# A planned kernel: from the fifth FFN unit on, the planner takes each weight block to land later

## Chip, cores, metric

One core of one Trainium2 chip runs the whole program in one launch. The metric is the device time of a run in microseconds (us); the time before is the median of three timed runs.

## The reference, cut to what matters

Three stages run on a tensor of 2 batches x 768 positions: windowed attention with sink tokens (8 heads of 64), then a mixture of four attention experts, then the stage that this change touches, a feed-forward mixture of eight experts that sends every position to one expert:

```python
logits = x @ w_gate                      # (2, 768, 8)
e      = routed expert of (b, s)         # argmax, or the previous position's expert by a local gate
h      = maximum(x[b, s] @ w1[e], 0)     # 512 -> 1024
out[b, s] = softmax(logits[b, s])[e] * (h @ w2[e])   # 1024 -> 512
```

## The kernel before

**The FFN stage.** The 1536 positions are sorted by expert into units of 128 rows, counted from 0. On this input, twelve units do the work: an expert has full units, and remainders of up to 32 rows go into one mixed batch (the pieces, `qw` weights, L1741). The twelve units belong to three experts: one has units 0 to 5, one has unit 6, one has units 7 to 11. Unit u does the following:

- a gather brings its rows (`xg`, L1563), TensorE transposes them (L1543), ScalarE and VectorE write them as `ux` in a high part (L1546) and a low part (L1550);
- its weights come as eight blocks of 512 KB, named (c, hf): c = 0, 1 are the two column halves of w1, c = 2, 3 the two row halves of w2, hf is the half of each. A block is loaded into its own `raw` buffer (`ld`, L1492, issued by SyncE, SP). Each of the eight has exactly one buffer, so unit u's load of a block waits until unit u-1's copy of it was split. The load is conditional: where unit u has the expert of unit u-1, nothing is moved and only the issue remains, so after unit 1 only units 6 and 7 move weights;
- every block is split: `hi` (ScalarE, L1507) rounds it to a high part, `lo` (VectorE, L1515) subtracts to get the low part; the split is done again in every unit. The results lie in eleven `w` buffers (their trace names are those of the tensors that once lived there: `w`, `wo_h`, `xT`, `wqk_h`, `wvg_h`);
- `unit_first`: 24 matmuls (three for each product, L315 to L317) into two banks, ScalarE's relu of each bank to `hs` (L1603), TensorE's transposes of `hs` (L1543), and high and low part of those, `hT` (L1546, L1550). These, with the output's scaling below, are a unit's evacuations: work that brings results out of PSUM;
- `unit_second`: 24 matmuls on `hT` with the c = 2, 3 blocks, ScalarE's scaling to `yo` (L1638), and a scatter to the output by GpSimd (L1641).

**What sets the order.** Tile's scheduler is off. Every piece of work is a `Task` with an engine, a duration, dependencies, buffers to acquire and release, and a priority (100 u plus an offset). `Order.run` is a list scheduler that works while the program is built: it asks `Order.ready` for the earliest start of each task, puts out the one that starts first (among equals the one with the lowest priority number), and advances that engine's clock. What it puts out is each engine's instruction order on the chip; its times are used for nothing else. `ready` takes the end of each dependency plus a latency; for a load (engine "DMA") the latency is 2.0, and a conditional load itself counts as `CLD` = 0.4:

```python
LAT = {"PE": 0.20, "ACT": 0.155, "DVE": 0.14, "POOL": 0.18, "DMA": 2.0, ...}
K["ld", u, c, hf] = add("DMA", CLD if u > 1 else 1.46, f, acq=[(("raw", 2 * c + hf), ...)], ...)
```

So the planner believes a block ready for its `hi` 2.4 after its load could start, whether or not the load moves anything. Units up to 10, and the front of unit 11, are one list; from unit 11 on, each unit is planned inside a branch on the number of units.

Of the kernel before, what the change touches and what calls it, by code (L numbers as in the profile page):

```python
# [32 lines left out]
RL = 1  # L33
PRP = 20
BPR = 120
BSP = 60
LAG1 = 0
ESP = 0.85
# [23 lines left out]
QN = 4  # L62
# [1 line left out]


class Task:
    __slots__ = ("eng", "dur", "fn", "deps", "acq", "rel", "prio", "end", "name", "rows", "fills", "lat")

    def __init__(self, eng, dur, fn, deps, acq, rel, prio, rows=False):
        self.eng, self.dur, self.fn, self.prio, self.rows = eng, dur, fn, prio, rows  # L70
        self.deps = [d for d in deps if d is not None]
        self.acq, self.rel = list(acq), list(rel)
        self.end = None
        self.fills = False
        self.lat = None


class Order:
# [17 lines left out]
    def add(self, eng, dur, fn, deps=(), acq=(), rel=(), prio=0, rows=False):  # L96
        t = Task(eng, dur, fn, deps, acq, rel, prio, rows)
        self.tasks.append(t)
        return t

    def ready(self, t):
        e = self.free.get(t.eng, 0.0)
        if t.eng == "PE" and t.rows != self.rows:
            e += self.TURN
        for d in t.deps:
            if d.end is None:
                return None
            e = max(e, d.end + (self.SAME.get(t.eng, 0.0) if d.eng == t.eng else d.lat or self.LAT[d.eng]))
        kinds = [a[0] for a in t.acq]
        for tag in set(kinds):  # L110
            free = sorted(x for x in self.slots.setdefault(tag, [0.0] * len(self.bufs[tag])) if x is not None)
            n = kinds.count(tag)
            if len(free) < n:
                return None
            e = max(e, free[n - 1])
        return e
# [54 lines left out]
def d_mr(n):  # L171
    return (n * 0.4375 + 8 if n >= 256 else 213) / 1000
# [14 lines left out]
def d_v(n):  # L187
    return (n / 0.96 + 65) / 1000


def d_a(n, extra=0):
    return (n / 1.2 + 52 + 93 * extra) / 1000
# [11 lines left out]
def fused_kernel(  # L204
# [106 lines left out]
    def f32(ap):  # L311
        return ap.bitcast(F32)
# [46 lines left out]
    if sinks:  # L359
# [4 lines left out]
        for r in range(3):  # L364
            t = bdm[32 * r:32 * r + 32]
# [1062 lines left out]
    def inv():  # L1428
        for j in range(T):
# [3 lines left out]
                   prio=END)  # L1433
# [4 lines left out]
        rel=["r_in"])  # L1438

    def spread(key, i):  # L1440
# [7 lines left out]
        rel=["r_q"])  # L1448
# [50 lines left out]
    def sp(u, c, hf, pr=None, ahead=False):  # L1499
        pool = (c, hf) in POOLW and u > 0 or ahead  # L1500
        pr = 100 * u + 5 * c + hf if pr is None else pr

        def hi():
            if ahead:
                nc.scalar.activation(R["w", u, c, hf][0], R["raw", u, c, hf], AF.Copy)
            else:
                nc.scalar.activation(R["w", u, c, hf][0], R["raw", u, c, hf], AF.Copy)  # L1507

        def lo():
            wh, wl = R["w", u, c, hf]  # L1510
            eng = nc.gpsimd if pool else nc.vector
            for k in range(PARTS if pool else 1):
                w_ = 512 // (PARTS if pool else 1)
                s_ = slice(k * w_, (k + 1) * w_)
                eng.tensor_sub(wl[:, :, s_], R["raw", u, c, hf][:, :, s_], f32(wh)[:, :, s_])  # L1515
        after = [K["ga", 1]] if u == 0 and (c, hf) == (3, 1) else []
        h = K["wh", u, c, hf] = add("ACT", d_a(1024) + 0.055, hi, deps=[K["ld", u, c, hf]] + (spent + [K["routed", JE]] * c if ahead else [K.get(("wh", 0, 1, 1))] * (u == 0 and c == 2)),
                                    acq=[("w", ("w", u, c, hf))], prio=pr)
        K["wl", u, c, hf] = add("POOL" if pool else "DVE", 2.4 + 0.07 * (PARTS - 1) if pool else d_v(1024), lo,
                                deps=[h] + after, prio=pr,  # L1520
                                rel=[("raw", u, c, hf)])
# [36 lines left out]
    def unit_front(u):  # L1558
        bp = base(u)

        def ga():
            xg = R["xg", u]
            nc.gpsimd.indirect_dma_start(out=xg, out_offset=None, in_=x2d if u else x2d[:JE * C, :],  # L1563
                                         in_offset=bass.IndirectOffsetOnAxis(ap=gix[:, u:u + 1] if u else gix0, axis=0))
        g0 = K["ga", u] = fo.add("POOL", 1.4, ga, deps=[K["gix"]] + [K["out", j] for j in range(T)] + [K.get("eui")] * (u > 1) if u else [K["gix0"]] + [K["out", j] for j in range(JE)] + [K["turnover"]],
                    acq=[("xg", ("xg", u))], prio=bp - 50 if u else at2((JE - 1) // NT, (JE - 1) % NT, E1) + RPO + 6)
        if u == 1:

            K["eui"] = fo.add("POOL", 0.1, lambda: nc.gpsimd.tensor_copy(eui[:32 + PC], euf[:32 + PC]), deps=[K["euf"], g0], prio=-49)
        for c in range(4 if u else 0):  # L1570
            for hf in range(2):
                ld(u, c, hf)
        g1 = fo.add("GD", 0.0 if u else 0.8, lambda: None, deps=[g0], prio=bp - 50)
        K["ux", u] = tr(("ux", u), lambda j: R["xg", u][:, j * 128:(j + 1) * 128], "ux", KD,
                        [g1] + ([K["g1", 0]] if u == 1 else []), bp - 40, [("xg", u)])
        for c in range(2 if u else 0):
            for hf in range(2):
                sp(u, c, hf)

    def unit_first(u):  # L1580
# [27 lines left out]
        for c in range(2, 4):  # L1608
            for hf in range(2 if u or c == 2 else 1):
                sp(u, c, hf, bp + 5 * c + hf + BSP if u else bp + 5 * c + hf - 48)  # L1610

    def unit_second(u, halves_=(0, 1)):
# [3 lines left out]
        for n in halves_:  # L1616
            for j0 in range(0, 4, step):
                def g2(n=n, j0=j0):
                    hh, hl = R["hT", u, n]
                    for j in range(j0, j0 + step):  # L1620
# [4 lines left out]
                g2s.append(fo.add("PE", 3 * step * d_mr(512), g2, deps=[K["hT", u, n], K["wl", u, 2 + n, hf]] + g2s,  # L1625
                                  acq=() if g2s else [("B", ("yp", u))], prio=bp + BPR + 4 * n + hf,
                                  rel=([("w", u, 2 + n, hf)] if (j0 + step) % 2 == 0 else []) + ([("hT", u, n)] if j0 + step == 4 else [])))
# [4 lines left out]
    def unit_end(u):  # L1632
# [7 lines left out]
        def sc_():  # L1640
# [5 lines left out]
            last_sc.append(sct)  # L1646
        e_ = fo.add("ACT", d_a(512), ev, deps=g2s + [K.get("pu")], acq=[("yo", ("yo", u))], rel=[("yp", u)], prio=bp + BPR + 10)
        f_ = fo.add("POOL", 1.1, sc_, deps=[e_], prio=bp + BPR + 10)
        fo.add("GD", 0.0, lambda: None, deps=[f_], rel=[("yo", u)], prio=bp + BPR + 10)

    n_ = len(order.tasks)
    unit_front(0)
    for c in range(4):
        if c == 1:
            behind = [K["ga", 0]]
        elif c == 2:
            behind = [K["ga", 0], K["out", T - DEFER]]
        for hf in range(2):
            ld(0, c, hf, END + c)
            if c < 2:  # L1660
                sp(0, c, hf, END + 40, True)
# [203 lines left out]
```

## Time and profile before

| | us |
|---|---|
| three timed runs: median (lowest to highest) | 424.39 (423.37 to 425.52) |
| the profiled execution: its time | 427.42 |
| its span, first to last instruction | 425.6 |
| outside the span | 1.8 |

TensorE has work for 403.8 us of the span, VectorE 336.2, ScalarE 326.6, GpSimd 173.6. The profiled execution is 3.0 us longer than the median of the timed runs. The FFN units fill the span from about 236 us to its end. A timeline row gives start, length, engine, line, what is written and read, and in brackets how long the engine stood idle before it and what ended that. Ends of matmuls are modelled: one that is followed at once by the next shows 0.39 us and starts 0.23 us before the next.

### The profile page before, as it was taken

What the parts mean: (1) busy time and instruction counts of PE and PEld (TensorE: products, weight loads), DVE (VectorE), ACT (ScalarE), POOL (GpSimd) and SP (SyncE); (2) the same over time, 40 slices, a digit from 0 to 9 for tenths busy, and PEclk for the clock granted to TensorE, in tenths of its full rate; (3) what the DMA queues carried; (4) which work ended last, traced back from release to release, by engine and by line L of the source; (5) the groups of instructions that cost most, each with busy time, mean ns of one, the idle gap of its engine ahead of it and who ended that gap; (6) DMA issues with size and microseconds to landing.
All of it is one profiled execution on the core that took longest, in us unless ns stands there. A gap on an engine that the chain in (4) does not pass through costs nothing.

```text
span 425.6 us, 10370 instructions
## 1 busy us (share of the span) xinstructions
PE 403.8 (95%) x3322; PEld 316.1 (74%) x3322; DVE 336.2 (79%) x959; ACT 326.6 (77%) x767; POOL 173.6 (41%) x270
## 2 busy tenths in 40 slices
PE   7899999999999997999999999999999699999994
PEld 3579979978779867979767677556566488888883
DVE  3999598697898789588799879476886779898690
ACT  5799799679999697765796438477695978989780
POOL 8289995198886358401642043111020401100101
PEclk9999999999999999999999999999999979999999
DMA  9997288645978445220910247786658971100011
GB/s 181 170 203 197 67 154 159 122 101 101 180 111 160 101 89 111 52 75 13 339 74 27 74 153 267 245 244 203 202 168 261 393 296 46 49 27 26 24 28 55
DMA packets 102046, 59.03 MB, mean 139 GB/s; under 512 B 84319, under 2 KB 85855, under 8 KB 101984
## 3 DMA queue, kind: packets, MB, share of 16 engines
q1 hardware_dynamic: 99824, 51.47, 48.7%
q0 software_dynamic: 2160, 6.82, 4.6%
q8 instruction: 28, 0.46, 0.5%
q14 instruction: 34, 0.28, 0.2%
HBM read 86.58 MB, written 6.55 MB: 219 GB/s over the span
## 4 chain that ended last, share of the span: by engine, by line
PE 49%; issue 24%; DVE 18%; POOL 4%; ACT 3%; SPq 1%; POOLq 0%; another core or an unknown queue 0%; DMA 0%; ACTq 0%; DVEq 0%
PE bank L315 8%; PE bank L317 8%; PE bank L316 8%; PE bank L685 6%; DVE P L699 4%; PE bank L809 3%; PE bank L1741 3%; PE bank L410 3%; DVE pT L816 2%; DVE PX L699 2%; POOL out_dram L1641 2%; PE bank L1140 1%; PE bank L1543 1%; PE bank L780 1%; PE bank L826 1%
## 5 line engine op out<-in xcount | busy, mean ns | idle before, releaser
L1515 DVE TENSOR_TENSOR w<-raw,w 128x1024 fp32r<-128x1024 f32 x44 | 52.9, 1221 | 13.8 <-ACT w L1507 13.6
L709 ACT ACTIVATE P<-P,nm 128x260 f32<-128x260 f32 (+3 forms) x100 | 53.1, 535 | 10.9 <-DVE nm L699 10.6
L1507 ACT ACTIVATE w<-raw 128x1024 fp32r<-128x1024 f32 x44 | 45.8, 1062 | 9.6 <-DMA raw<-in_moe_w_dram 8.3
L769 POOL TENSOR_TENSOR raw<-PX,raw 128x512 f16<-128x512 f32 (+2 forms) x34 | 35.5, 1050 | 15.8 <-ACT raw L764 13.9
L1641 POOL DMA_INDIRECT out_dram<-yof,six x12 | 13.0, 1085 | 67.4 <-ACT yof L1638 66.2
L816 DVE TENSOR_TENSOR pT<-bank,pT 128x512 f16<-128x512 f32 (+1 forms) x50 | 30.7, 631 | 9.4 <-ACT pT L812 9.3
L1563 POOL DMA_INDIRECT xgf<-x2d,gix x9 | 10.4, 1152 | 66.3 <-PE bank L1543 60.8
L685 PE MATMUL bank<-kT,qT 64*128 64x260 f32 (+1 forms) x192 | 31.5, 398 | 2.1 <-POOL kT L583 1.1
L709 ACT ACTIVATE PX<-PX,nm 128x260 f32<-128x260 f32 (+4 forms) x60 | 30.5, 510 | 1.4 <-DVE nm L699 1.3
L315 PE MATMUL bank<-xT,wqk_h 128*128 128x256 f32 x96 | 29.5, 307 | 0.0
L410 PE MATMUL bank<-ident,raw 128*128 128x128 f32 x168 | 28.0, 289 | 0.5 <-DVE raw L949 0.3
L812 ACT ACTIVATE pT<-bank 128x512 f16<-128x512 f32 (+1 forms) x50 | 26.1, 550 | 2.8 <-PE bank L809 2.5
L809 PE MATMUL bank<-ident,P 128*128 128x128 f32 x180 | 26.8, 277 | 1.0 <-ACT P L709 0.7
L317 PE MATMUL bank<-xT,wqk_l 128*128 128x256 f32 x96 | 27.8, 289 | 0.0
L316 PE MATMUL bank<-xT,wqk_h 128*128 128x256 f32 x96 | 27.7, 288 | 0.0
L699 DVE CUSTOM_DVE_ANT_0 P<-bank,mask 128x260 f32<-128x260 f32 (+1 forms) x60 | 22.3, 399 | 5.4 <-POOL mask L332 4.7
L685 PEld LDWEIGHTS bank<-kT,qT 64*128 64x128 f32 x192 | 19.2, 185 | 9.2 <-issue 2.3
L1603 ACT ACTIVATE hs<-bank 128x512 f32<-128x512 f32 x24 | 14.3, 596 | 15.3 <-PE bank L317 15.3
L646 POOL TENSOR_SCALAR raw<-raw,s_sv 128x256 f32<-128x256 f32 x20 | 18.4, 930 | 18.0 <-ACT qT L416 9.1
L410 PEld LDWEIGHTS bank<-ident,raw 128*128 128x128 f32 x168 | 20.1, 162 | 7.0 <-DVE nm L699 2.0
L685 PE MATMUL bank<-k,q 64*128 64x256 f32 (+3 forms) x128 | 24.4, 466 | 0.1
L1515 DVE TENSOR_TENSOR xT<-raw,xT 128x1024 fp32r<-128x1024 f32 x16 | 19.2, 1217 | 6.6 <-ACT xT L1507 6.4
(456 smaller groups left out, 1476.8 us busy)
## 6 DMA issues: line engine op xcount, KB each, us to landing
raw<-in_moe_w_dram SPq DMA_DIRECT2D x104, 512.0 KB
qw<-in_moe_w_dram SPq DMA_DIRECT2D x64, 256.0 KB
raw<-in_v_dram SPq DMA_DIRECT2D x12, 256.0 KB
x2d<-x SPq DMA_DIRECT2D x12, 256.0 KB
raw<-in_q_dram SPq DMA_DIRECT2D x11, 256.0 KB
raw<-in_k_dram SPq DMA_DIRECT2D x11, 256.0 KB
pT<-raw SPq DMA_TRANSPOSE x46
raw<-in_moe_wv_dram SPq DMA_DIRECT2D x1, 512.0 KB
```

What stands on the lines that cost most here:

```text
L315: nc.tensor.matmul(o, l[0], r[0], start=start, stop=False)
L316: nc.tensor.matmul(o, l[0], r[1], start=False, stop=False)
L317: nc.tensor.matmul(o, l[1], r[0], start=False, stop=stop)
L410: nc.tensor.transpose(p[:, j * 128:(j + 1) * 128], src(j), ident)
L685: nc.tensor.matmul(o, l, r, start=True, stop=True)
L699: nc.vector.tensor_tensor_reduce(p, s, sg["mask"], 0.0 if dead and st == 1 else -scale, gr["nm"] if si else 3.0e38, op0=OP.add, op1=OP.min ...
L709: nc.scalar.activation(p, p, AF.Exp, bias=gr["nm"], scale=-1.0, accum_out=sg["sum"]())
L769: nc.gpsimd.tensor_sub(shaped(pl[:, s_], dims), p_, shaped(ph[:, s_], dims))
L809: nc.tensor.transpose(R[tk][:, j * 128:(j + 1) * 128], R[gr["P"]][:, c:c + 128], ident)
L816: nc.vector.tensor_sub(pl[:, :n * 128], R[tk][:, :n * 128], ph[:, :n * 128])
L1507: nc.scalar.activation(R["w", u, c, hf][0], R["raw", u, c, hf], AF.Copy)
L1515: eng.tensor_sub(wl[:, :, s_], R["raw", u, c, hf][:, :, s_], f32(wh)[:, :, s_])
```

## The change

A task gets a new field, `slack`, which `ready` adds to the end of each of its dependencies. It is 0 for all tasks but the `hi` of the weight blocks of units 5 and up (`QN` is 4), where it is 6.0; a `hi` has one dependency, its load. So the planner now counts such a block as ready 8.4, and not 2.4, after its load could start. No instruction is added or removed, and no wait: only the order in which the planner puts them out can differ.

```diff
+LATE = 6.0
...
+        self.slack = 0.0
...
-            e = max(e, d.end + (self.SAME.get(t.eng, 0.0) if d.eng == t.eng else d.lat or self.LAT[d.eng]))
+            e = max(e, d.end + t.slack + (self.SAME.get(t.eng, 0.0) if d.eng == t.eng else d.lat or self.LAT[d.eng]))
...
         h = K["wh", u, c, hf] = add("ACT", d_a(1024) + 0.055, hi, deps=[K["ld", u, c, hf]] + ..., prio=pr)
+        if u > QN:
+            h.slack = LATE
```

## Rows read from the trace of the kernel before

**Rows 1.** The page's busy time, share of the span, instructions.
```profile
PE 403.8 (95%) x3322; PEld 316.1 (74%) x3322; DVE 336.2 (79%) x959; ACT 326.6 (77%) x767; POOL 173.6 (41%) x270
```

**Rows 2.** Busy time by stretch: engines, then granted clock, DMA share, GB/s.
```profile
312.50:325.00 12.50, 12.50 (x68) 8.99 (x66) 12.25 (x12) 10.82 (x14) 2.60 (x2) 1.00 0.65 208
...
329.90:339.10 9.20, 6.16 (x29) 4.38 (x28) 7.07 (x8) 8.79 (x12) 3.60 (x3) 1.00 1.05 393
339.10:346.00 6.90, 6.26 (x15) 4.96 (x16) 5.13 (x6) 4.65 (x6) 0.87 (x1) 0.51 1.05 393
346.00:358.40 12.40, 12.40 (x62) 10.18 (x61) 11.28 (x11) 10.48 (x14) 2.00 (x2) 1.00 0.33 119
...
383.20:395.60 12.40, 12.40 (x62) 10.20 (x61) 11.29 (x12) 11.16 (x15) 0.98 (x1) 1.00 0.06 22
```

**Rows 3.** TensorE's timeline, units 4 to 6, 315 to 355 us.
```profile
315.25 0.60 PE L1543 MATMUL bank<-ident,xgf 128*128 128x128 f32 x4
...
319.12 0.40 PE L315 MATMUL bank<-wo_h,uxf 128*128 128x512 f32 x1
...
324.64 0.60 PE L1543 MATMUL bank<-ident,hs 128*128 128x128 f32 x4
325.17 1.92 PE L1741 MATMUL bank<-qw,v2l 128*32 128x512 f32 x16
...
331.25 0.66 PE L1543 MATMUL bank<-ident,hs 128*128 128x128 f32 x4 [1.18 <-ACT hs L1603]
...
338.35 0.50 PE L315 MATMUL bank<-wo_h,ux 128*128 128x512 f32 x1 [1.83 <-ACT ux L1546]
...
339.74 0.80 PE L317 MATMUL bank<-wo_h,ux 128*128 128x512 f32 x1 [0.67 <-DVE ux L1550]
...
346.13 0.39 PE L317 MATMUL bank<-w,ux 128*128 128x512 f32 x1
...
354.65 0.39 PE L315 MATMUL bank<-w,uxf 128*128 128x512 f32 x1
```

**Rows 4.** ScalarE's timeline, 322 to 338 us.
```profile
322.72 0.60 ACT L1603 ACTIVATE hs<-bank 128x512 f32<-128x512 f32 x1
326.60 1.06 ACT L1507 ACTIVATE wo_h<-raw 128x1024 fp32r<-128x1024 f32 x1 [3.28 <-DMA raw<-in_moe_w_dram]
329.65 1.06 ACT L1507 ACTIVATE w<-raw 128x1024 fp32r<-128x1024 f32 x1 [1.99 <-DMA raw<-in_moe_w_dram]
330.62 0.58 ACT L1603 ACTIVATE hs<-bank 128x512 f32<-128x512 f32 x1
...
332.98 1.06 ACT L1507 ACTIVATE w<-raw 128x1024 fp32r<-128x1024 f32 x1 [0.28 <-DMA raw<-in_moe_w_dram]
...
337.70 0.60 ACT L1546 ACTIVATE ux<-bank 128x512 fp32r<-128x512 f32 x1
```

**Rows 5.** ScalarE's timeline, 314 to 317 us: unit 5's first splits.
```profile
314.09 1.05 ACT L1507 ACTIVATE wo_h<-raw 128x1024 fp32r<-128x1024 f32 x1
...
315.99 0.68 ACT L1638 ACTIVATE yof<-bank,pu 128x512 f32<-128x512 f32 x1
```

**Rows 6.** VectorE's timeline: low parts of units 5 and 6.
```profile
315.63 1.22 DVE L1515 TENSOR_TENSOR wo_l<-raw,wo_h 128x1024 fp32r<-128x1024 f32 x1
...
327.70 1.23 DVE L1515 TENSOR_TENSOR wo_l<-raw,wo_h 128x1024 fp32r<-128x1024 f32 x1 [2.30 <-ACT wo_h L1507]
```

**Rows 7.** SP's load issues for units 6 and 7, in three windows.
```profile
321.33 2.60 SPq L1492 DMA_DIRECT2D raw<-in_moe_w_dram  x3
...
324.35 3.96 SPq L1492 DMA_DIRECT2D raw<-in_moe_w_dram  x5
...
333.67 2.54 SPq L1492 DMA_DIRECT2D raw<-in_moe_w_dram  x3
```

**Rows 8.** ScalarE's timeline, splits of units 7 and 8.
```profile
340.07 1.07 ACT L1507 ACTIVATE w<-raw 128x1024 fp32r<-128x1024 f32 x1
...
368.58 1.06 ACT L1507 ACTIVATE wqk_h<-raw 128x1024 fp32r<-128x1024 f32 x1 [0.30 <-PE bank L317]
```

More of the change, by code (lines that the diff above doesn't have):

```diff
@@ L66 @@
 class Task:
-    __slots__ = ("eng", "dur", "fn", "deps", "acq", "rel", "prio", "end", "name", "rows", "fills", "lat")
+    __slots__ = ("eng", "dur", "fn", "deps", "acq", "rel", "prio", "end", "name", "rows", "fills", "lat", "slack")
     def __init__(self, eng, dur, fn, deps, acq, rel, prio, rows=False):
```

## The prediction

> **What bounds the kernel now.** I read the page first: TensorE has work for 95% of the span [rows 1]. Then the table by stretch [rows 2], cut at unit boundaries counted back from the twelve output scalings: TensorE is full from 312 us to 325 and again from 346 to the tail, where a unit takes 12.40 us, all of it TensorE. The exception is 329.9 to 346: first 6.16 us of work in 9.20, then a stretch at a granted clock of 0.51, the lower of the two levels (1.2 of 2.4 GHz). Third, TensorE's timeline there [rows 3]: three waits, 1.18 for a relu, 1.83 and 0.67 for `ux`, all for ScalarE or for VectorE behind it. Fourth, ScalarE's timeline [rows 4]: why these are late. Unit 5's second relu reads a bank that is complete when TensorE goes on to the transposes at 324.64 [rows 3], yet it starts at 330.62. ScalarE stands 3.28 and 1.99 us at the heads of unit 6's splits of blocks (0, 0) and (0, 1), whose loads have not landed. The relu, `hT` (its transposes done since 325.2) and later `ux` are queued behind them. The weights are late and the evacuations are not; the order makes both late.
>
> **Part 1, the order of unit 6's splits.** The planner puts `hi` of block (0, 0) of unit 6 ahead of the second relu, because it counts the load as 0.4 + 2.0. On the chip, the load is issued at 321.33 [rows 7] and its split starts at 326.60: 5.3 us instead of 2.4. With 8.4 the `hi` becomes ready in the plan after the second relu, both `hT` high parts and the pieces' output, which take two to five planned us; so I expect ScalarE to have, in this order: relu 1 of unit 5, the rest of unit 5's splits, relu 2, `hT` 1, the pieces' scaling, `hT` 2, then unit 6's (0, 0), (0, 1), (1, 0) with unit 4's scaling and `ux` between. What this removes:
> - the three waits, 1.18 + 1.83 + 0.67 = 3.68 us [rows 3]. By the modelled ends each hides another 0.16 (a matmul's row lasts 0.39, the next starts after 0.23), which would make it 4.2;
> - the half clock. From 339.74 to 346.13 TensorE starts 15 matmuls [rows 2, 3]: 6.39 us. At the 0.23 us between starts of the full stretches (24 matmuls of unit 5 in 5.52 us, 319.12 to 324.64) they are 3.47. The difference is 2.92 us, and it goes if the clock fell because of the three waits right ahead of it.
>
> Gross 3.68 + 2.92 = 6.60, with the hidden part 7.1 at most.
>
> The Trainium skill (TensorE: Matmul & The Clock Gate, section "Why this matters for your kernels") lays the fall to the lower clock on a long idle gap between bursts of matmuls. The longest here is 1.83 us and matmuls run between the three, so I doubt that it would call these the cause; by that rule the clock's 2.92 would stay lost, and the sum would be 3.68. But the clock fell at 339.10, as the third wait began [rows 2, 3], after nothing else than these waits: I go by the row.
>
> **Part 2, unit 5's splits.** They wait 6 more as well, though their loads move nothing (same expert as unit 4). Before, (0, 0), at 314.09, and (0, 1) stand ahead of unit 3's scaling at 315.99 [rows 5]. I expect scaling and `ux` first. The scaling must wait for unit 3's last matmul, which `ux`'s transposes follow at 315.25 [rows 3], so its end is at about 315.4. Scaling (0.68) and `ux` follow, and the splits begin at about 316.5: 2.4 us later. The low part of (0, 0), 315.63 to 316.85 before [rows 6], then ends near 319.0. What hides it: the planner, seeing unit 5's matmuls not ready, takes six matmuls of unit 4's second half and eight of the pieces' sixteen (1.92 us from 325.17 before [rows 3]) ahead; both come after unit 5's matmuls before. That is 1.4 + 1.0 = 2.4 us of TensorE work, so unit 5's first matmul, 319.12 before, comes at 321.5 with its block ready 2.5 us earlier. If that cover were missing, up to 2.4 us is paid. Cost: 0. Unit 5's `lo` free the `raw` buffers for unit 6; the ones that matter end by 322.3, and SP issues these loads from 321.33 at 0.8 to 1.0 us each in any case [rows 7]. SP's order itself doesn't change: the pieces' last loads are planned ahead of unit 6's as before. GpSimd's scatters and gathers keep their order and aren't waited for here.
>
> **Part 3, what is late next.** Following TensorE by hand from 321.5: unit 5's 24 matmuls to 327.1 (relu 1 at 324.4), its transposes, the second eight of the pieces to 328.6, unit 4's last twelve to 331.8, `ux` transposes to 332.2, twelve matmuls of unit 5 to 335.0. ScalarE: relu 2 at 327.2, `hT` 2 done at 330.0, then unit 6's (0, 0) at 330.0 (326.60 before), (0, 1) at 331, (1, 0) at 332, scaling, `ux` at 333.5 (337.70 before); VectorE's `ux` at 335.3. If nothing fills, TensorE stands 0.5 us there; six more matmuls of unit 5 are ready and can. So the cost is 0 to 0.5, and I take 0.5 against the 0.5 hidden in the modelled ends: net 6.6 us.
>
> Unit 6's weights are all there by then. Unit 7's loads wait for the `raw` of unit 6: (0, 0) was issued behind the `lo` at 327.70 to 328.93 [rows 6], and would now wait for one that ends near 332.4, 3.1 us later; the next ones, from 333.67 [rows 7], waited for `lo` that hardly move, the fourth by about 1 us. Unit 7's first matmuls move to 348 from 354.65 [rows 3]. The fourth of its blocks, issued near 337, lands within 5.3 us like unit 6's first, or 8.6 like its fourth (issued at 324.35 [rows 7], split at 332.98 [rows 4]) as the DMA engines are full there [rows 2]: 342.3 to 345.6; its split takes 1.06 + 1.22 more. It is wanted eighteen matmuls into the unit, at 348 + 4.2. Margin about 4 us, cost 0.
>
> **Part 4, the later units.** From unit 7 on, splits wait for a `w` buffer that TensorE frees [rows 8], and a unit is 12.40 us of TensorE [rows 2]. The planned cycle of one `raw` buffer is 8.4 + 0.96 + 1.13 + 0.30 = 10.8 by the constants in the code, under that 12.4; so the plan falls back to the old order within about three units, and in between splits stand some 5 us later than before, against a lead of 14 over their use (340.07 to 354.65 [rows 3, 8]). Cost 0; ScalarE and VectorE have 1.1 to 1.2 us to spare a unit [rows 2]. The tail is left as it is.
>
> **Sum.** The profiled execution goes from 427.42 to 420.8, its span from 425.6 to 419.0. It ran 3.0 over the median of the timed runs; I take the same 6.6 us off that: 424.39 - 6.6 = 417.8.
>
> **Rivals.**
> - *The clock's share does not come.* The waits go, but the fall has another cause, or the timed runs (3.0 us shorter than the profiled one, about the price of the half clock) never had it. Against it: the fall stands right behind the waits [rows 2, 3]. Gain 3.7, time 420.7.
> - *A new wait takes the place.* The relu's wait becomes one for unit 6's `ux` or weights, which come at 330 to 335 by DMA and VectorE whatever the order: VectorE takes 1.22 us a split [rows 6] and is busy 12.25 of 12.5 us [rows 2] ahead of it. If `ux` is put four splits later on VectorE, 4.9 us are given back, and with over half of the clock's share lost again (1.7 us) the time is 424.4 - 6.6 + 4.9 + 1.7 = 424.4: within 0.5%.
> - *Unit 7's loads become the bound*, the one that ends slower. Its sixteen-block run with unit 6 fills the DMA engines (393 GB/s [rows 2]). If the chain `lo` of unit 6, free `raw`, load, `hi`, `lo` holds TensorE at unit 7, its start keeps its old time plus the 3.1 us by which its first load is issued later: 354.65 + 3.1, time 427.5. It decides from the point where the fourth block lands after about 350; I have it at 342 to 346. It would also leave TensorE idle for several us, with a new half clock.
>
> The Trainium skill (DMA: Bandwidth & Descriptors, "Where 436 GB/s comes from") has loads from HBM bound at about 358 GB/s for a core; the stretch above shows 393, so the measurement decides, and by the page's figure the sixteen blocks would take 2 us more, an estimate, which speaks a little for this rival.
>
> **Chances and range.** Forecast 0.62; clock's share missing 0.16; new wait 0.12; unit 7's loads 0.10. The forecast alone spans 416 (7.1 and a little, if the timed runs lose more than the profiled one) to 420. A change under 0.5% (2.1 us) is about what a measurement of this kernel can't tell from none. Faster by more: 0.62 + 0.16 = 0.78; within: 0.12; slower: 0.10. For 8 in 10, the range takes in the forecast, the missing clock and part of the new wait: 415.5 to 423.5.
>
> **What the profile would show.** Right: ScalarE's relu 2 of unit 5 and both its `hT` stand ahead of unit 6's `wo_h`; ScalarE's waits for `raw` shrink from 5.6 us in all (3.28 + 1.99 + 0.28 [rows 4]) to under 1; TensorE's waits between 315 and 345 sum to under 0.6; no stretch at half clock there; 12.40 us a unit from unit 7 on. Part 2 is wrong if TensorE waits at unit 5's first matmul; part 3 if it waits for `ux` or `w` at units 6 or 7; part 4 if a unit after 7 takes over 12.5. The prediction fails above all if the waits move to VectorE's `ux`, or if the half clock stays with the waits gone.

## Result and the profile after

Timed side by side, the changed kernel takes 420.48 us (median of 22 runs) where the kernel before takes 424.77 (22 runs). The ratio is 0.9904 [0.9876, 0.9933], a gain of 4.1 us (2.8 to 5.3). The forecast was 417.8. The ratio, and every mean over runs below, leaves out the runs that lie over 1.5% above the fastest of their kernel; of the changed kernel's 22 these are four, at mean granted clocks of 0.986 to 0.990, and over all 22 and 22 the means differ by 3.7 us and the medians by 4.3.

The profiled execution took 422.84 us, with a span of 421.1. The page's busy time, against [rows 1], hardly moves:

```profile
PE 401.7 (95%) x3322; PEld 314.6 (75%) x3322; DVE 335.8 (80%) x959; ACT 325.1 (77%) x767; POOL 174.8 (42%) x270
```

The table by stretch, as in [rows 2] (us of the stretch, busy time of TensorE, its weight loads, VectorE, ScalarE and GpSimd, then granted clock, DMA share, GB/s):

```profile
312.50:325.00 12.50, 12.50 (x75) 7.39 (x74) 11.05 (x12) 10.76 (x14) 1.99 (x2) 1.00 0.65 194
...
329.90:339.10 9.20, 9.20 (x51) 6.86 (x50) 8.06 (x10) 8.74 (x12) 3.46 (x3) 1.00 1.03 381
339.10:346.00 6.90, 6.90 (x36) 5.68 (x34) 6.50 (x7) 6.01 (x9) 0.00 (x0) 1.00 1.05 392
346.00:358.40 12.40, 12.40 (x62) 10.20 (x61) 12.03 (x13) 11.75 (x16) 3.31 (x2) 1.00 0.51 187
383.20:395.60 12.40, 12.40 (x62) 10.17 (x61) 11.75 (x12) 10.90 (x15) 1.28 (x1) 1.00 0.06 22
```

The two stretches that had holes are full: 9.20 of 9.20 where 6.16 was busy, and 36 matmul rows at full clock in 6.90 us where 15 ran at 0.51. The DMA engines are as full as they were. TensorE's list of waits from 250 us to the end (line, what it waited for, us in total, times, longest) holds two, both ahead of 300 us; the three of [rows 3] are gone:

```profile
PE bank L318 <- DVE w L1517: 0.4, 1, 0.4
PE bank L1789 <- DVE v2l L1783: 0.2, 1, 0.2
```

ScalarE's timeline through units 5 and 6. Lines stand two to four higher in the changed file: L1507 is L1509, L1603 is L1607, L1546 is L1550, L1638 is L1642.

```profile
317.95 0.69 ACT L1642 ACTIVATE yof<-bank,pu 128x512 f32<-128x512 f32 x1 [1.25 <-PE bank L319]
318.54 0.59 ACT L1550 ACTIVATE uxf<-bank 128x512 fp32r<-128x512 f32 x1
319.02 1.06 ACT L1509 ACTIVATE wo_h<-raw 128x1024 fp32r<-128x1024 f32 x1
...
327.24 0.60 ACT L1607 ACTIVATE hs<-bank 128x512 f32<-128x512 f32 x1 [2.43 <-PE bank L319]
...
329.97 0.60 ACT L1607 ACTIVATE hs<-bank 128x512 f32<-128x512 f32 x1 [0.24 <-PE bank L319]
330.46 0.59 ACT L1550 ACTIVATE hT<-bank 128x512 fp32r<-128x512 f32 x1
331.45 0.69 ACT L1756 ACTIVATE yof<-bank,puq 128x512 f32<-128x512 f32 x1 [0.39 <-PE bank L1745]
332.03 0.59 ACT L1550 ACTIVATE hTf<-bank 128x512 fp32r<-128x512 f32 x1
332.51 1.06 ACT L1509 ACTIVATE xT<-raw 128x1024 fp32r<-128x1024 f32 x1
...
335.36 0.69 ACT L1642 ACTIVATE yof<-bank,pu 128x512 f32<-128x512 f32 x1
335.93 0.60 ACT L1550 ACTIVATE ux<-bank 128x512 fp32r<-128x512 f32 x1
```

The idle times in brackets say what changed. In [rows 4] ScalarE stood for loads (`raw`), with evacuations queued behind. Now it stands only for TensorE's banks, which nobody pays for: both `hs` start at the end of their matmuls, and unit 6's first split (332.51) follows the second `hT` and finds its data there.

TensorE's timeline at the same places:

```profile
317.76 0.60 PE L1547 MATMUL bank<-ident,xgf 128*128 128x128 f32 x4
...
324.10 0.50 PE L317 MATMUL bank<-wo_h,uxf 128*128 128x512 f32 x1
...
329.71 0.60 PE L1547 MATMUL bank<-ident,hs 128*128 128x128 f32 x4
330.24 1.06 PE L1745 MATMUL bank<-qw,v2l 128*32 128x512 f32 x8
331.24 0.66 PE L1547 MATMUL bank<-ident,hs 128*128 128x128 f32 x4
```

Two scales are needed to compare the two traces. The transposes of unit 5's `ux` start at 317.76 here and at 315.25 in [rows 3], so 2.5 us are taken off the times of after. And the **stage**, from these transposes to the end of the span, is 425.6 - 315.25 = 110.35 before and 421.1 - 317.76 = 103.34 after: 7.0 us shorter, though the span is only 4.5 shorter. The first 315 us were 2.5 us longer in this execution; further executions below show such shifts in both kernels.

### The profile page after: what moved, and what is told of

It is laid out like the page before. It is cut to its first block, busy times and chain, and to the rows that moved or that the text cites. A ratio compares the mean times of both kernels' runs of the same rounds, so it can differ in the third digit from the quotient of the medians.

```text
span 421.1 us, 10369 instructions
## 1 busy us (share of the span) xinstructions
PE 401.7 (95%) x3322; PEld 314.6 (75%) x3322; DVE 335.8 (80%) x959; ACT 325.1 (77%) x767; POOL 174.8 (42%) x270
## 4 chain that ended last, share of the span: by engine, by line
PE 51%; issue 22%; DVE 16%; POOL 4%; ACT 4%; DMA 1%; POOLq 0%; another core or an unknown queue 0%; ACTq 0%; DVEq 0%
PE bank L317 9%; PE bank L319 8%; PE bank L318 8%; PE bank L687 6%; DVE P L701 3%; PE bank L811 3%; PE bank L1745 3%; PE bank L412 3%; DVE PX L701 2%; DVE pT L818 2%; POOL out_dram L1645 2%; DMA pT<-raw 1%; PE bank L1547 1%; PE bank L1142 1%; PE bank L828 1%
## 5 line engine op out<-in xcount | busy, mean ns | idle before, releaser
L1517 DVE TENSOR_TENSOR w<-raw,w 128x1024 fp32r<-128x1024 f32 x43 | 51.4, 1219 | 11.7 <-ACT w L1509 11.7
L1509 ACT ACTIVATE w<-raw 128x1024 fp32r<-128x1024 f32 x43 | 44.3, 1062 | 6.9 <-DMA raw<-in_moe_w_dram 6.7
L1645 POOL DMA_INDIRECT out_dram<-yof,six x12 | 13.8, 1152 | 65.8 <-ACT yof L1642 64.6
L1517 DVE TENSOR_TENSOR xT<-raw,xT 128x1024 fp32r<-128x1024 f32 x18 | 21.7, 1216 | 6.8 <-ACT xT L1509 6.8
L1607 ACT ACTIVATE hs<-bank 128x512 f32<-128x512 f32 x24 | 14.3, 594 | 16.4 <-PE bank L319 16.2
```

## Experiments

The theory: ScalarE's evacuations were stuck behind unit 6's splits, TensorE stood 3.7 us for them, and the lower clock followed from its standing. Against it stand three others: that the clock has another cause, or is absent from most runs; that the gain comes from another part (unit 5's splits, or the later units'); and that another amount than 6.0 would do as well, since any delay of the splits lets the evacuations through.

The table sums up the runs; the stage is as above, and waits are TensorE's in it. The last two columns are means over runs. *Clock loss* is (1 - mean granted clock) x span, the most that the lower clock can have cost that run, wherever in the run it fell; *the rest* is the time less that. The row of before holds the runs that were timed beside the experiments, with before_b and before_c (for the 22 of the result no clock is on record); ± is a 95% interval of the mean.

| kernel | ratio to before [95%] | stage, us | waits, us | clock loss | the rest |
|---|---|---|---|---|---|
| before (63 runs) | 1 | 110.35, 107.85, 108.4 | 3.7, 3.9, 3.1 | 3.2 ± 0.3 | 421.2 ± 0.3 |
| after (19) | 0.9904 [0.9876, 0.9933] | 103.3, 103.3 | 0, 0 | 1.7 ± 0.5 | 418.5 ± 0.5 |
| u6on (6) | 0.9891 [0.986, 0.9921] | 103.1 | 0 | 2.6 ± 0.8 | 418.1 ± 1.1 |
| u6only (12) | 0.9955 [0.9921, 0.999] | 104.6 | 1.2 | 2.0 ± 0.7 | 420.5 ± 0.7 |
| u5only (12) | 1.001 [0.9977, 1.0042] | 107.55 | 3.4 | 2.5 ± 0.9 | 422.1 ± 0.8 |
| fill (12) | 0.9986 [0.9955, 1.0016] | 106.8 | 0 | 1.2 ± 0.3 | 422.8 ± 0.5 |
| late3 (11) | 0.9977 [0.9941, 1.0012] | 106.5 | 2.2 | 2.1 ± 1.0 | 421.1 ± 0.8 |
| late9 (10) | 1.0055 [1.0026, 1.0084] | 110.8 | 2.4 | 2.8 ± 1.0 | 424.2 ± 0.7 |
| late12 (6) | 1.0599 [1.0541, 1.0656] | 134.3 | 14.2 | 11.9 ± 1.1 | 438.7 ± 1.0 |

### Which unit's splits matter: u6only, u5only, u6on

The change with its condition narrowed: to unit 6 alone, to unit 5 alone, and to units 6 and up.

```diff
-        if u > QN:
+        if u == QN + 2:      # u6only
+        if u == QN + 1:      # u5only
+        if u > QN + 1:       # u6on
```

> The 6.0 is given to unit 6's splits alone. Theory 1 (all of the gain comes from unit 6's splits no longer standing ahead of unit 5's relu and copies): the three waits of TensorE between 329 and 340 us and the half clock behind them are gone as in the changed kernel, 7.0 us less in the profile from unit 5's ux transposes to the end, and the same timed ratio as the changed kernel, 0.990. Theory 2 (the gain needs the matmuls that unit 5's later splits let go ahead): one wait of 1 us or more stays, the ratio lies between 0.993 and 1.0.

> The 6.0 is given to unit 5's splits alone. Unit 6's block (0, 0) is then planned ahead of even the first relu of unit 5, and that relu waits for the load. Theory 1: no gain; ScalarE waits for the load at 321 to 327 us with the relu behind it, TensorE waits at unit 5's transposes, 1 to 4 us in all, and the half clock comes; ratio 0.998 to 1.01. Theory 2 (unit 5's part carries the gain): ratio under 0.995.

> The 6.0 for units 6 and up, not for unit 5. Theory 1 (what counts is that the splits of the two units that load, 6 and 7, stand behind the unit before's relu and copies; unit 6 alone left one wait of 1.2 us at unit 6's second relu, behind unit 7's loads): no wait of TensorE between 315 and 400 us, 103.3 to 103.8 us from unit 5's ux transposes to the end as in the changed kernel, ratio 0.990 to 0.992. Theory 2 (unit 5's part is needed as well): one or more waits stay, 104.5 us or more, ratio 0.994 to 0.997.

Unit 6 alone keeps about half of the gain: 422.81 us against 424.98. Its one wait of the stage stands a unit later than before's. ScalarE's timeline:

```profile
339.24 1.06 ACT L1509 ACTIVATE wo_h<-raw 128x1024 fp32r<-128x1024 f32 x1 [0.62 <-DMA raw<-in_moe_w_dram]
341.17 1.06 ACT L1509 ACTIVATE w<-raw 128x1024 fp32r<-128x1024 f32 x1 [0.87 <-DMA raw<-in_moe_w_dram]
342.13 0.58 ACT L1607 ACTIVATE hs<-bank 128x512 f32<-128x512 f32 x1
```

and TensorE's row that waits for it:

```profile
342.76 0.66 PE L1547 MATMUL bank<-ident,hs 128*128 128x128 f32 x4 [1.17 <-ACT hs L1607]
```

It is the same pattern one unit on: unit 7 moves weights too, its splits wait for loads, and unit 6's second relu is queued behind them. So unit 7's splits need the delay as well. Its ratio of 0.9955 is in theory 2's range, but not for that theory's reason, the matmuls that unit 5's splits let go ahead. Unit 5 alone gains nothing. TensorE waits 1.1 us for unit 5's first relu, which is behind a split of unit 6, and 2.2 for unit 6's second, which is behind splits of unit 7. ScalarE's rows of the former:

```profile
327.39 1.06 ACT L1509 ACTIVATE w<-raw 128x1024 fp32r<-128x1024 f32 x1 [5.54 <-DMA raw<-in_moe_w_dram]
328.35 0.58 ACT L1607 ACTIVATE hs<-bank 128x512 f32<-128x512 f32 x1
```

The half clock that u5only's theory 1 expected did not come: 3.4 us of waits, some 20 us apart, and its profile has the full clock from 312 us to TensorE's last matmul.

Units 6 and up give all of it (420.46 us, no wait in the stage), and the interval of u6on covers the change's own ratio: the delay of unit 5's splits is worth nothing that can be measured, as Part 2 had it. No version here is clearly better than the change.

### The clock by itself: fill, before_b, before_c

*fill* is the kernel before with matmuls in place of the waits: five ahead of unit 5's second transposes, eleven ahead of unit 6's first matmul. Their results are overwritten by the matmuls that follow.

```diff
+            if key == ("hT", 5, 1):
+                wf = R["w", 4, 3, 1][0]
+                for _ in range(5):
+                    nc.tensor.matmul(p, wf[:, 0, :128], wf[:, 0, :], start=True, stop=True)
...
+                    if u == 6 and n == 0 and d0 == 0:
+                        wf = R["w", 6, 0, 0][0]
+                        for _ in range(11):
+                            nc.tensor.matmul(R["hp", u, n], wf[:, 0, :128], wf[:, 0, :], start=True, stop=True)
```

> The kernel before, with 5 and 11 matmuls more on TensorE just ahead of the two instructions that wait (1.18 us and 1.83 + 0.67 us); their results are overwritten. They fill the waits and take no wait away. If the half clock comes of the three waits: the clock stays at 1.00 to the end of the matmuls, and the profile is 2.9 us shorter from unit 5's ux transposes to the end; timed ratio 0.993 where every run of before has the half clock, less where not. If the clock falls for another reason: it falls again at about 339 us and the time is that of before, ratio 0.999 to 1.002.

It has no wait in the stage and full clock there (the stretch against 0.51 in [rows 2]):

```profile
329.00:339.00 10.00, 10.00 (x50) 8.23 (x49) 8.42 (x10) 9.35 (x14) 4.38 (x3) 1.00 1.05 392
339.00:346.00 7.00, 7.00 (x37) 5.69 (x35) 6.14 (x6) 5.65 (x8) 0.00 (x0) 1.00 1.05 394
```

Yet its time is that of before within 0.5%: 0.6 us less (1.9 less to 0.7 more). Either the clock costs nothing like 2.92 in most runs, or the sixteen matmuls (16 x 0.23 = 3.7 us) cost more than the waits that they fill. Two more executions of the kernel before, unchanged, tell how often the clock falls:

> The kernel before, unchanged, for its profile. Theory 1 (the three waits are in every run and the half clock behind them by chance, so that the timed runs have gained little more than the waits): the waits sum to 3.5 to 3.9 us again, and in this profile or the next the clock stays up at 340 us, where the time from unit 5's ux transposes to the end is 107.5 us and not 110.4. Theory 2 (each run has the half clock; the timed gain is smaller for something else): both show it, 110.4.

> The kernel before, unchanged, a second time. As for the first: by theory 1 107.5 or 110.4 us from unit 5's ux transposes to the end, as the clock falls or not; by theory 2 110.4.

before_b, TensorE's waits from 312 to 345 us:

```profile
PE bank L315 <- ACT ux L1546: 1.7, 1, 1.7
PE bank L1543 <- ACT hs L1603: 1.5, 1, 1.5
PE bank L317 <- DVE ux L1550: 0.7, 1, 0.7
```

and two stretches of it:

```profile
339.00:346.00 7.00, 7.00 (x35) 5.57 (x34) 6.07 (x6) 5.66 (x9) 0.00 (x0) 1.00 1.05 392
360.00:421.80 61.80, 55.78 (x269) 45.54 (x267) 45.02 (x45) 44.52 (x58) 7.96 (x8) 0.98 0.10 36
```

before_c, the waits of the same 33 us:

```profile
PE bank L315 <- ACT ux L1546: 2.4, 1, 2.4
PE bank L317 <- DVE ux L1550: 0.7, 1, 0.7
```

and its stretches:

```profile
329.00:339.00 10.00, 6.92 (x33) 5.07 (x32) 8.61 (x9) 8.77 (x12) 4.38 (x3) 0.97 1.05 392
339.00:346.00 7.00, 7.00 (x28) 5.66 (x27) 5.74 (x6) 4.99 (x7) 0.00 (x0) 0.80 1.05 394
```

Behind almost the same waits, one instruction order had the stretch of 6.8 us at half clock [rows 2], one of half that length (0.97 over 10 us, then 0.80 over 7) and none. One profile is one draw.

The runs listed with their granted clock give the mean, but two parts of the column are not the stage's waits. One is the end of the run: before_b's mean clock is 0.997, so its loss is 0.003 x 421.8 = 1.3 us, and the row from 360 us accounts for it (0.02 x 61.8 = 1.2). There TensorE's last matmul ends at 415.8 us and the clock falls at 419.1, so this part costs nothing. All profiles have it. The other lies ahead of the stage. Every profile has one wait of TensorE near 168 us, for VectorE's `r_ms` in the attention part, 1.4 to 2.1 us long, which the change does not touch; in six of the twelve the clock falls at about its end, and in two more it falls at 212 and 222 us. In the profile of the changed kernel (its row, then its stretch, then the same stretch before):

```profile
169.78 0.58 PE L1287 MATMUL bank<-ident,r_ms 128*1 128x128 f32 x2 [2.04 <-DVE r_ms L1283]
...
168.00:173.00 5.00, 3.23 (x16) 3.13 (x17) 4.14 (x13) 1.80 (x7) 2.39 (x3) 0.67 0.67 129
...
168.00:173.00 5.00, 5.00 (x30) 4.85 (x29) 3.76 (x20) 3.79 (x14) 1.16 (x1) 0.66 0.63 121
```

Before and fill are the same program at both places, so the column can be compared between these two: before loses 3.2 us in a run and fill 1.2, so the waits of the stage bring 2.0 us of lower clock in the mean. 46 of 63 runs of before have a mean clock of 0.994 or less, and 0 of 12 of fill. So lower clock does follow from the stage's waits, and the timed runs do have it, at less than the one profile showed. For the changed kernel the column settles less. 5 of its 19 runs have a mean clock of 0.994 or less (9 of all 23, with a mean loss of 2.4 ± 0.7), though neither of its profiles has a wait or a fall between the stage's start and TensorE's last matmul; the first, at 0.993, has the fall shown above. Where its other runs lost their clock is not on record.

That fill wins only 0.6 is on the other column: its rest is 1.6 us over before's. Where its matmuls overshoot the waits (before_c had no wait for `hs` at all) they are paid; that this makes up the 1.6 was not measured.

The Trainium skill (TensorE: Matmul & The Clock Gate, "Why this matters for your kernels") lays a drop in mid-kernel on a long idle gap between bursts of matmuls. The gaps here are 0.7 to 2.4 us, so these runs show falls that this rule does not name: with the gaps filled, fill's profile has no fall in the stage, and none of its twelve runs has a mean clock under 0.995.

### How much delay: late3, late9, late12

```diff
-LATE = 6.0
+LATE = 3.0      # late3
+LATE = 9.0      # late9
+LATE = 12.0     # late12
```

> 3.0 in place of 6.0. The second relu of unit 5 and its first hT are planned ahead of unit 6's block (0, 0), but ux of unit 6 stands behind six of unit 6's splits and not three. Theory 1 (what costs is standing behind a load that has not landed; once the splits start at 327 us or later the loads are there): no wait over 0.5 us between 315 and 345 us, 103.3 to 104 us from unit 5's ux transposes to the end, ratio 0.989 to 0.992. Theory 2 (ux needs the full 6.0 as well): a wait of 1.5 us or more for ux stays ahead of unit 6's first matmul, ratio 0.993 to 0.997.

3.0 is too little. TensorE's waits of the stage:

```profile
PE bank L1547 <- ACT hs L1607: 1.6, 2, 1.2
PE bank L319 <- DVE hTf L1554: 0.6, 1, 0.6
```

and ScalarE's rows ahead of the longest:

```profile
345.84 1.06 ACT L1509 ACTIVATE w<-raw 128x1024 fp32r<-128x1024 f32 x1 [0.33 <-DMA raw<-in_moe_w_dram]
346.80 0.58 ACT L1607 ACTIVATE hs<-bank 128x512 f32<-128x512 f32 x1
```

Neither theory held. Unit 5's evacuations come through, but unit 6's relus are again behind unit 7's splits, which wait for loads. It is not `ux` that is late next. About a quarter of the gain is left (1.0 us of 4.1), and the interval includes none.

> 9.0 in place of 6.0: the planned cycle of one weight buffer is 13.8, between the 12.4 us of TensorE in a unit and the 16.8 of the run with 12.0, where a unit took 17.3 on the chip. Theory 1 (the chip follows the plan once the planned cycle passes TensorE's 12.4): units of 13.8 to 14.2 us from unit 6 on, 9 us more than the changed kernel, ratio 1.007 to 1.015. Theory 2 (the loss at 12.0 is that of a plan that overshoots far, 9.0 is still filled on the chip): units of 12.4, ratio 0.988 to 0.993.

> The 6.0 is doubled to 12.0. The planned cycle of one weight buffer is then 16.8, over the 12.4 us of TensorE in a unit, and the planner puts each unit's second matmuls wholly ahead of the next unit's first. Theory 1 (the change costs nothing later only because its cycle of 10.8 is under 12.4): TensorE waits 1.5 to 2.5 us in each of units 5 to 10 for its own relu and hT with nothing to fill in; 430 to 436 us, ratio 1.015 to 1.03. Theory 2 (later is as good: the planned times don't reach the chip): as the changed kernel, ratio 0.988 to 0.992.

Both lose, late9 a little less than its theory 1 said (1.007 to 1.015) and late12 twice as much and more (1.015 to 1.03). By Part 4's sum the planned cycle of one `raw` buffer is 13.8 with 9.0 and 16.8 with 12.0, over TensorE's 12.4 a unit. late9, one unit (out of 372.78 to 386.25), TensorE 12.99 busy of 13.47:

```profile
372.78:386.25 13.47, 12.99 (x63) 10.21 (x61) 10.97 (x12) 10.70 (x15) 0.98 (x1) 1.00 0.06 21
```

late12, one unit:

```profile
372.69:390.00 17.31, 14.82 (x62) 11.20 (x61) 11.20 (x12) 10.92 (x15) 0.99 (x1) 0.90 0.04 15
```

and TensorE's rows in it:

```profile
381.48 0.49 PE L317 MATMUL bank<-w,ux 128*128 128x512 f32 x1 [1.72 <-ACT w L1509]
382.74 0.79 PE L318 MATMUL bank<-w,ux 128*128 128x512 f32 x1 [0.77 <-DVE w L1517]
383.33 0.63 PE L319 MATMUL bank<-w,ux 128*128 128x512 f32 x1
```

The units that move no weights (15 GB/s here) now run at about the planned cycle, 13.5 and 17.3 us, because the plan has laid each split behind evacuations of the unit before, and the chip keeps that order. In late12 the split that TensorE wants at 381.48 stands behind a scaling for which ScalarE itself was idle 4.28 us:

```profile
379.80 0.69 ACT L1642 ACTIVATE yof<-bank,pu 128x512 f32<-128x512 f32 x1 [4.28 <-PE bank L319]
380.38 1.99 ACT L1509 ACTIVATE w<-raw 128x1024 fp32r<-128x1024 f32 x2
```

TensorE then stands for the split, not for the relu and `hT` as expected: 1.72 for ScalarE's part and about 0.77 for VectorE's, in five units, and the lower clock (0.63 us a matmul in place of 0.39) follows each time: the mean loss is 11.9 us, 8.7 over before's. late9 shows almost no wait on TensorE for its 1.1 us a unit: the list has 2.4 us for the whole stage, and the rest of what a unit is longer is not accounted for by it.

### The changed kernel again: after_b

> The changed kernel, unchanged, for a second profile. Theory 1 (the clock falls only where TensorE waits, and by chance): no wait of TensorE and no half clock between 315 and 410 us again, 103.2 to 103.6 us from unit 5's ux transposes to the end. Theory 2 (the first profile was a lucky one): a wait or a half clock there, 104.5 us or more.

after_b took 419.18 us. Its stage is 417.5 - 314.18 = 103.3 us, that of the first profile to 0.1, with no wait. So the stage repeats, and the 315 us ahead of it, where no instruction of TensorE stands elsewhere, vary: 317.76 and 314.18 for the changed kernel, 313.95 to 315.25 for before.

## Why the prediction was right, and where it was off

**Right: what bounds it and Part 1.** ScalarE's order is the one listed, and the times, less 2.5 us, are those worked out by hand: second relu 327.5 (327.2 forecast), unit 6's (0, 0) at 330.0 (330.0), `ux` at 333.4 (333.5). The waits for loads on ScalarE are gone, TensorE's three too. u6only and u5only show that it was the order of the splits of units that load. Unit 7's must be delayed as well once unit 6's are, which Part 1 did not price.

**Right: Part 2.** Unit 5's first matmul comes at 324.10 - 2.5 = 321.6 (321.5 forecast), with matmuls of unit 4 and of the pieces ahead of it and no wait. u6on leaves this part out, and its time is the same.

**Right: Part 3.** No wait at `ux` or at unit 7 in either profile of the changed kernel. The rival of unit 7's loads is out: these splits stand later, and units 7 and on take 12.40.

**Right: Part 4, with less room than it seemed.** 12.40 us a unit, as the planned cycle of 10.8 against 12.4 said. late9 and late12 show the other side of that comparison, where the change would have been slower.

**The step that was off: the sum's second term, the half clock at 2.92 us.** It was read from one profile and counted as if every run had it. Against the stage of that one profile the forecast is good: 7.0 us came out where 6.6 was forecast and 7.1 was the most. In the timed runs the clock loss fell by 3.2 - 1.7 = 1.5 us, half of 2.92, and by 1.0 if no run is left out (3.4 - 2.4). fill put what the stage's waits bring at 2.0, so not all of that was seen to go. The profile's own mean clock of 0.987 is a loss of 5.5 us, 2.3 over the mean run; that is most of the 3.0 us by which it was longer than the median, and the sum took the 6.6 off the median all the same. Some 1.7 of the 5.5 (5.00 x 0.34) stand at 168 to 173 us, out of the change's reach. The first term is off by less: the waits were 3.1 to 3.9 us in three profiles, and the rest fell by 421.2 - 418.5 = 2.7 ± 0.6. 1.5 + 2.7 is 4.2, the difference of the means.

**The rival "the clock's share does not come"** gave the time nearest to the measured one, 420.7 against 420.48, but not for its reason: part of the clock came, and part of the waits' 3.68 did not show. The new wait did not appear in the changed kernel; it did in u6only and late3, in another place than the rival had it.

**Open.** Why the clock falls in one run and not in the next behind the same waits. Where the changed kernel's runs of low mean clock lose it. Why the profiles of the stage (3.4 to 4.6 us shorter with the clock's share taken out: 107.85 without any half clock, and 110.35 and 108.4 less half of their 6.8 and 3.4 us at half clock, against 103.3) say somewhat more than the rest of the timed runs, 2.7. And what besides the listed waits makes late9's unit 1.1 us longer.

## What to carry to other kernels

Where a planner fixes an in-order engine's queue, count a load as landing when the trace says it lands, or the queue's head waits and everything behind it waits too; and check the planned cycle of each buffer against the unit time, because a delay that exceeds it slows the units behind it, loaded or not. Price a clock that falls by chance from the granted clock of many runs, not from one profile: (1 - mean clock) x span is the most that it can cost in a run. See in the profiles where it falls: here one part fell when TensorE had nothing left to do, and another ahead of all that the change moves. Before taking a profile's stall off a median, ask whether the stall is why the profiled run is longer than the median.

## What the runs showed of the hardware that was not expected

- Waits of 0.7 to 2.4 us, 3.1 to 3.9 in all within 10 us, had 6.8, 3.4 and 0 us of the lower clock with or behind them in three executions of one kernel; with the same places filled, no run of twelve had a mean clock under 0.995. In late12, two waits of 1.7 and 0.8 us brought it in each unit that was looked at (0.90 to 0.91 over a unit). Behind the one wait near 168 us it came in six of twelve profiles, and in u5only, behind waits of 1.1 and 2.2 us some 20 us apart, not at all.
- The start of the stage moved between 313.95 and 317.76 us from execution to execution under the same instruction order ahead of it.
